# Turning twelve of sixteen row blocks by transposing DMA instead of on TensorE, in a fused LayerNorm + spectral filter + GeGLU kernel

## The chip, the cores and the metric

The kernel runs on one core of a Trainium2 chip. A core has five engines that run their own instruction streams and meet at semaphores: TensorE (PE, matmuls and transposes, results in PSUM), VectorE (DVE), ScalarE (ACT), GpSimd (POOL) and SyncE (SP, which here only issues DMA transfers). The metric is the device time of one execution in microseconds; three runs of the kernel before gave 176.29, 176.81 and 177.09 us.

## The reference

```python
xn = _layernorm(x, axis=-1)                       # x: (1, 2048, 512) bf16, eps 1e-5, no scale or bias
X  = rfft2(xn.astype(float32), axes=(-2, -1))     # over 2048 tokens and 512 features
y  = irfft2(X * (w_r + 1j * w_i), s=(2048, 512))  # w_r, w_i: (2048, 257)
g, u = xn @ w_gate, xn @ w_up                     # (512, 1792) each
h  = gelu_tanh(g) * u
out = x + y + h @ w_down                          # w_down: (1792, 512)
```

Two branches read the same normalised rows: a two-dimensional spectral filter and a gated MLP. Their results and x are added.

## The kernel before, in words

The 2048 tokens are 16 rows of 128 tokens (a "row" below is such a block, 128 tokens on the partitions by 512 features), and four rows make a chunk. For each row, VectorE takes the statistics (`stats`, lines 524 and 525), the reciprocal root of the variance comes from GpSimd (`root_pool`, lines 536 and 537; the first row's from ScalarE), and VectorE writes the normalised row into one of eight buffers in `specB` (`norm`, line 541). Roots are taken for four rows at a time from row 4 on.

Everything that follows wants the features on the partitions, so each normalised row is turned (`turn`, lines 543 to 559): TensorE transposes four 128x128 blocks per row into PSUM (line 554), and VectorE copies the result into `xnT` (line 559). From row 4 on two rows are turned at a time.

From `xnT` two things start. The MLP branch: `gated` makes, for a chunk and each of 14 blocks of hidden features, a gate group and an up group of four matmuls each (line 679); ScalarE takes gelu and a copy out of PSUM, VectorE multiplies (line 686), and `down` makes one row of output from 14 hidden blocks (line 724). The first chunk is done in smaller pieces at the start (`first`, line 698). The spectral branch: `fold` (VectorE) adds and subtracts mirrored features of a chunk, TensorE transforms pairs of rows along the features (line 593), ScalarE empties PSUM (line 598). When all four chunks are there, VectorE does the upper part of the token transform, TensorE the rest (lines 813 and 816), VectorE multiplies by the filter `W` in `filt` (line 472, with the edge columns at lines 826 and 860), and the inverse runs back the same way (lines 893, 894, 953) into x.

The filter comes from HBM in two halves: near rows, loaded straight from `w_r` and `w_i`, and mirror rows, which are first copied in reverse order from HBM into a scratch tensor in HBM (`w_mirror`) and then loaded from there. `tf` and `ti` are tables for the forward and inverse token transforms.

The order of instructions on each engine is written by a planner in the file (`_Sched`): every operation has an engine, a cost, a key or due time, and for transfers a size that is charged to one common pipe at `RATE`; the planner simulates and fixes each engine's order, and semaphore waits follow from what reads and writes what. So the orders of all engines shift when costs, keys or operations change. `STAT` and `NORM` set due times of statistics and norms of rows 4 to 15. Operations with a key over 1000, the MLP's matmuls, fill TensorE wherever nothing else is ready. `gate` is a list of operations that every later SyncE transfer must wait for.

All loads but three small ones go through SyncE's one queue, in this order: x, gate and up weights, small tables, the rest of x, `w_down`, `tf`, `ti`, the six reversing copies, the near filter rows, single rows of the filter, and the loads from the scratch.

Of the kernel before, what the change touches and what calls it, by code (L numbers as in the profile page):

```python
# [15 lines left out]
P = 128  # L16
NFC = 14
# [2 lines left out]
WARM = 8  # L20
HKEY = 1.5
NORM = 14.0, 1.5
STAT = 13.0, 1.6
SLACK = 0.05
MARGIN = 1.0
RATE = 340e3
# [120 lines left out]
class _Sched:  # L147
# [11 lines left out]
    def op(self, eng, cost, fn, reads=(), writes=(), tiles=(), key=0.0, after=(), dma=0, lag=0.0, due=None):  # L159
        o = _Op()  # L160
        o.eng, o.fn, o.cost, o.key, o.dma, o.lag, o.due = eng, fn, cost, key, dma, lag, due
        o.reads, o.writes, o.tiles = reads, writes, [(t, False) for t in tiles]
        o.extra = [a for a in after if a is not None]
        o.seq = len(self.ops)
        o.end = None
        o.pos = None
        self.ops.append(o)
        return o
# [182 lines left out]
def bass_parallel_sum__spectral_gfnet__glu_gated_geglu__prompt_kernel(  # L351
# [13 lines left out]
    c_ti = nc.inline_tensor(ti_np, name="c_ti")  # L365
# [9 lines left out]
    wdv = B_w_down.rearrange("(fc p) d -> p fc d", p=P)  # L375

    sch = _Sched()
    op = sch.op

    with ExitStack() as es:  # L380
        def sb(name, shape, dt=BF16, cell=0):
            n = int(np.prod(shape))
            t = es.enter_context(nc.sbuf_tensor(name, [P, n], dt))
            return view(t, name, 0, shape, cell)
# [14 lines left out]
        xnT = sb("xnT", [4, 4, 4, P])  # L399
        wg = sb("wg", [4, FF])  # L400
        wu = sb("wu", [4, FF])
        wd = sb("wd", [NFC, D])
        small = sb("smallc", [11, P])
        tf = sb("tokf", [18, P])
        ti = sb("toki", [8, 3, P])
        W = sb("filt", [2, 2, 8, 257], cell=1)
        w1 = sb("filt1024", [2, 512])
# [56 lines left out]
        gate = []  # L464

        def dma(q, dst, src, nbytes, wr=None, rd=None, key=0.0, after=(), cost=0.41, lag=0.0):
            after = tuple(after) + tuple(gate if q == "sp" else ())
            return op(q, cost, lambda e: e.dma_start(dst() if callable(dst) else dst.ap, src() if callable(src) else src.ap),  # L468
                      reads=rd if rd is not None else (), writes=wr if wr is not None else (), dma=nbytes, key=key, after=after, lag=lag)
# [7 lines left out]
        def load(q, dst, src, nbytes, **kw):  # L477
            return dma(q, dst, lambda: src, nbytes, wr=(dst,), **kw)
# [4 lines left out]
        k = iter(np.arange(0.0, 1.0, 0.001))  # L483
        first_row = None
        for s in range(4):
            for part, rows in halves(A_x, SL[s]):
                o = load("sp", x[part, s], rows, 1024 * (part.stop - part.start), key=next(k))
# [45 lines left out]
        def root_pool(s0, n, key):  # L533
            sl = slice(s0, s0 + n)
            v, y, h = vv[:, sl], rs[:, sl], half[:, sl]
            op("pool", 0.2 + 0.03 * n, lambda e: e.tensor_scalar(v.ap, bag.ap[:, sl, 1], LN_EPS, None, ADD), reads=(bag[:, sl],), writes=(v,), key=key)
            op("pool", 0.5 + 0.14 * n, lambda e: e.tensor_tensor(y.ap, v.ap, h.ap, ALU.pow), reads=(v, h), writes=(y,), key=key)

        def norm(s, key, due=None):
            o, i = xn(s).rs([512]), xs(s)  # L540
            op("dve", 0.34, lambda e: e.tensor_scalar(o.ap, i.ap, bag.ap[:, s, 0:1], rs.ap[:, s:s + 1], SUB, MUL),
               reads=(i, bag[:, s], rs[:, s:s + 1]), writes=(o,), key=key, due=due)

        def turn(s0, n, key):
            b, sl = s0 // 4, s0 % 4
            t = _T("sp")

            def bank():
                return ps_sp_bf[:, t.slot * 2048:t.slot * 2048 + 512 * n]

            def f(e):
                ins = None
                for i in range(4 * n):
                    ins = e.transpose(bank()[:, i * P:(i + 1) * P], xn(s0 + i // 4).ap[:, i % 4], ident.ap)  # L554
                return ins

            o = xnT[:, b, sl:sl + n].rs([512 * n])
            op("pe", 4 * n * 0.056, f, reads=tuple(xn(s0 + i) for i in range(n)) + (ident,), tiles=(t,), key=-40, lag=0.1)
            op("dve", 0.08 + n * 0.26, lambda e: e.tensor_copy(o.ap, bank()), writes=(o,), tiles=(t,), key=key)  # L559


        Y = R1(0, [16, D])
        H = R3(0, [16, D])
# [53 lines left out]
        fold(0)  # L617
        for s in range(4, 16):
            stats(s, 0.0, STAT[0] + STAT[1] * (s - 4))
            if s % 4 == 3:  # L620
                root_pool(s - 3, 4, -4.0)
        for s in range(4, 16):
            norm(s, 0.0, NORM[0] + NORM[1] * (s - 4))
            if s % 2 == 1:
                turn(s - 1, 2, 1.0)
            if s % 4 == 3:
                fold(s // 4)


        load("sp", wd, wdv, NFC * 131072, key=next(k))  # L630
        load("sp", tf, c_tf.ap().rearrange("p (t m) -> p t m", t=18), 589824, key=next(k))
        load("sp", ti, c_ti.ap().rearrange("p (v t q) -> p v t q", v=8, t=3), 786432, key=next(k))
        scr, far, near = {}, {}, {}
        for ri, src in ((0, A_w_r), (1, A_w_i)):
            c16 = src.rearrange("(m c) k -> c m k", c=16)
# [2 lines left out]
                dma("sp", lambda ri=ri: scr[ri][0:4], lambda c16=c16: c16[12:16, ::-1, :], 526336, key=next(k), cost=3.5, lag=6.0),  # L638
                dma("sp", lambda ri=ri: scr[ri][5:8], lambda c16=c16: c16[5:8, ::-1, :], 394752, key=next(k), cost=2.5, lag=6.0)]
            near[ri] = dma("sp", lambda ri=ri: scr[ri][4:9:4, 0:64], lambda c16=c16: c16[0:9:8, 127:63:-1, :], 131584, key=next(k), cost=2.0, lag=5.0)  # L640
        for ri, src in ((0, A_w_r), (1, A_w_i)):
            r16 = src.rearrange("(m c) k -> m c k", c=16)
            load("sp", W[0:64, ri, 0, 0], r16[0:64, 0], 32896, key=next(k))
            load("sp", W[64:P, ri, 0, 0], r16[0:64, 8], 32896, key=next(k))
            load("sp", W[:, ri, 0, 1], r16[:, 4], 65792, key=next(k))
            for c in (1, 2, 3):
                load("sp", W[:, ri, 0, 2 * c:2 * c + 2], r16[:, c:c + 9:8], 131584, key=next(k))
            load("sp", W[0:1, ri, 1, 0], r16[0:1, 0], 514, key=next(k))
        for ri in (1, 0):
            load("sp", W[1:64, ri, 1, 0], scr[ri][4, 0:63], 32382, after=(near[ri],), key=1.0 + next(k))  # L650
            load("sp", W[64:P, ri, 1, 0], scr[ri][8, 0:64], 32896, after=(near[ri],), key=1.0 + next(k))
            load("sp", W[:, ri, 1, 1], scr[ri][0], 65792, after=(far[ri][0],), key=1.0 + next(k))
            for c in (1, 2, 3):
                load("sp", W[:, ri, 1, 2 * c:2 * c + 2], scr[ri][4 - c::4][0:2].rearrange("c m k -> m c k"), 131584, after=tuple(far[ri]), key=1.0 + next(k))
        op("pool", 0.1, lambda e: e.memset(w1[0:1].ap, 0.0), writes=(w1,))
        for dst, src, lo, hi in ((w1[0:1, 0, 0:256], A_w_r, 0, 256), (w1[0:1, 0, 257:512], A_w_i, 1, 256),
                                 (w1[0:1, 1, 1:256], A_w_i, 1, 256), (w1[0:1, 1, 257:512], A_w_r, 1, 256),
                                 (w1[0:1, 1, 256:257], A_w_r, 256, 257)):
            load("sp", dst, src[1024:1025, lo:hi], 512, key=next(k))


        fill = [0]
# [143 lines left out]
        for v, hh in enumerate(((14, 15), (12, 13), (0, 1), (4, 6), (8, 9), (10, 11), (2, 7), (5, 3))):  # L806
            t = _T("sp")
# [17 lines left out]
        for ri, f in ((0, ADD), (1, SUB)):  # L825
            op("pool", 0.3, lambda e, ri=ri, f=f: e.tensor_tensor(edge.ap[:, ri], ev[0].ap[:, ri], ev[1].ap[:, ri], f),
               reads=(ev[0][:, ri], ev[1][:, ri]), writes=(edge[:, ri],), key=1.0)
# [53 lines left out]
        for v in range(8):  # L881
            t = _T("sp")

            def f_i(e, v=v, t=t):
# [15 lines left out]
               writes=(gv,), tiles=(t,), key=-0.5)  # L900
# [40 lines left out]
        for jq in range(4):  # L941
# [4 lines left out]
            for jp in (2 * jq, 2 * jq + 1):  # L946
                t = _T("sp")
# [57 lines left out]
```

## Time and profile before

| | before |
|---|---|
| time, median of 3 runs | 176.81 us (176.29 to 177.09) |
| the profiled execution | 177.05 us |
| its span | 175.3 us |
| TensorE busy | 170.2 us, 97% |
| VectorE busy | 146.4 us, 84% |
| ScalarE busy | 106.2 us, 61% |
| GpSimd busy | 11.3 us, 6% |
| granted TensorE clock | 1.00 |

The span runs from the first to the last instruction that the profiler saw; the execution's time holds 1.7 us around it. The chain of work that ended last is followed back from the last instruction, each time to what released it. In rows of groups and timelines, an operation is given as line, engine, operation, output<-input, shape; "<-" at the end names what ended the idle time before it. In a timeline the first two columns are start and duration in microseconds; neighbouring instructions of one kind are merged. SPq is SyncE's own queue of DMA issues; its durations are those of issuing, not of the transfers. In rows of windows, the columns are the window, its length, busy time and instruction count of TensorE, its weight loads, VectorE, ScalarE and GpSimd, then the granted clock, the busy share of the 16 DMA engines and GB/s.

### The profile page before, as it was taken

What the parts mean: (1) busy time and instruction counts of PE and PEld (TensorE: products, weight loads), DVE (VectorE), ACT (ScalarE), POOL (GpSimd) and SP (SyncE); (2) the same over time, 40 slices, a digit from 0 to 9 for tenths busy, and PEclk for the clock granted to TensorE, in tenths of its full rate; (3) what the DMA queues carried; (4) which work ended last, traced back from release to release, by engine and by line L of the source; (5) the groups of instructions that cost most, each with busy time, mean ns of one, the idle gap of its engine ahead of it and who ended that gap; (6) DMA issues with size and microseconds to landing.
All of it is one profiled execution on the core that took longest, in us unless ns stands there. A gap on an engine that the chain in (4) does not pass through costs nothing.

```text
span 175.3 us, 2759 instructions
## 1 busy us (share of the span) xinstructions
PE 170.2 (97%) x1042; PEld 89.8 (51%) x1042; DVE 146.4 (84%) x289; ACT 106.2 (61%) x172; POOL 11.3 (6%) x19
## 2 busy tenths in 40 slices
PE   7789999999999999999999999999999999999994
PEld 2578654555665444444444464554445564444443
DVE  3769999999819999976999999969999939982931
ACT  3378756567598375987636395794636896562000
POOL 2220302200000034000000000000000000000000
DMA  5999998222455530000000000000000001410311
GB/s 153 280 358 356 351 357 306 65 61 54 70 110 118 136 92 0 4 0 0 0 2 0 4 0 0 0 4 0 0 0 2 4 0 52 128 60 4 120 60 62
DMA packets 17805, 14.77 MB, mean 84 GB/s; under 512 B 1151, under 2 KB 17408, under 8 KB 17792
## 3 DMA queue, kind: packets, MB, share of 16 engines
q1 hardware_dynamic: 16592, 13.75, 26.7%
q10 hardware_dynamic: 1200, 0.85, 1.6%
q8 instruction: 8, 0.13, 0.3%
q14 instruction: 5, 0.04, 0.1%
HBM read 12.50 MB, written 3.15 MB: 89 GB/s over the span
## 4 chain that ended last, share of the span: by engine, by line
PE 92%; DMA 4%; SPq 1%; issue 0%; DVE 0%
PE ps_gu L679 54%; PE ps_dn L724 21%; PE ps_sp L724 7%; DMA wu<-in_B_w_up_dram 3%; PE ps_sp L593 3%; PE ps_sp L953 2%; PE ps_sp L554 2%; PE ps_sp L813 2%; DMA x_sb<-in_A_x_dram 1%; SPq L468 1%; PE ps_sp L893 1%; PE ps_sp L894 1%; PE ps_sp L816 0%; DVE x_sb L735 0%
## 5 line engine op out<-in xcount | busy, mean ns | idle before, releaser
L679 PE MATMUL ps_gu<-xnT,wu 128*128 128x512 bf16 (+1 forms) x236 | 56.7, 363 | 0.7 <-DMA wu<-in_B_w_up_dram 0.7
L679 PE MATMUL ps_gu<-xnT,wg 128*128 128x512 bf16 (+1 forms) x236 | 56.7, 363 | 0.0
L684 ACT ACTIVATE gg<-ps_gu 128x512 bf16<-128x512 f32 (+1 forms) x59 | 33.8, 573 | 13.8 <-PE ps_gu L679 12.5
L685 ACT ACTIVATE uu<-ps_gu 128x512 bf16<-128x512 f32 (+1 forms) x59 | 33.9, 575 | 12.8 <-PE ps_gu L679 12.3
L724 PE MATMUL ps_dn<-wd,hT 128*128 128x512 bf16 x168 | 38.9, 379 | 0.0
L679 PEld LDWEIGHTS ps_gu<-xnT,wu 128*128 128x128 bf16 x236 | 22.7, 98 | 22.9 <-ACT gg L684 0.9
L679 PEld LDWEIGHTS ps_gu<-xnT,wg 128*128 128x128 bf16 x236 | 22.6, 98 | 21.8 <-DVE xnT L559 0.3
L472 DVE TENSOR_TENSOR specB<-specB 128x1024 bf16<-128x1024 bf16 (+2 forms) x47 | 29.2, 659 | 1.5 <-ACT specB L958 1.4
L724 PEld LDWEIGHTS ps_dn<-wd,hT 128*128 128x128 bf16 x168 | 16.4, 98 | 19.6
L686 DVE TENSOR_TENSOR hT<-gg,uu 128x512 bf16<-128x512 bf16 (+1 forms) x59 | 22.3, 391 | 1.9 <-ACT uu L685 1.9
L732 ACT ACTIVATE db<-ps_dn 128x512 bf16<-128x512 f32 x12 | 7.2, 597 | 19.8 <-PE ps_dn L724 19.8
L472 DVE TENSOR_TENSOR specB<-specA 128x2048 bf16<-128x2048 bf16 x8 | 9.4, 1220 | 6.5 <-ACT specA L598 3.9
L524 DVE BATCH_NORM_STATS2 bst<-x_sb 128x6 f32<-128x512 bf16 x16 | 10.9, 682 | 3.8 <-DMA x_sb<-in_A_x_dram 3.6
L472 DVE TENSOR_TENSOR specC<-specB 128x1024 bf16<-128x1024 bf16 (+5 forms) x21 | 12.5, 628 | 0.1
L724 PE MATMUL ps_sp<-wd,hT 128*128 128x512 bf16 (+2 forms) x70 | 12.3, 336 | 0.0
L724 PEld LDWEIGHTS ps_sp<-wd,hT 128*128 128x128 bf16 x70 | 6.3, 98 | 6.1 <-DVE x_sb L735 0.2
L472 DVE TENSOR_TENSOR specB<-specB,filt 128x2048 bf16<-128x2048 bf16 x8 | 9.4, 1215 | 0.0
L821 ACT ACTIVATE specA<-ps_sp 128x1024 bf16<-128x1024 f32 x8 | 8.0, 1024 | 2.2 <-PE ps_sp L816 1.8
L733 DVE TENSOR_TENSOR x_sb<-db,x_sb 128x512 bf16<-128x512 bf16 x12 | 5.0, 415 | 4.4 <-ACT db L732 4.4
L958 ACT ACTIVATE specB<-ps_sp 128x1024 bf16<-128x1024 f32 x8 | 7.8, 1031 | 0.8 <-PE ps_sp L953 0.8
L598 ACT ACTIVATE specA<-ps_sp 128x1024 bf16<-128x1024 f32 x8 | 8.0, 1046 | 0.1
L899 ACT ACTIVATE specC<-ps_sp 128x1024 bf16<-128x1024 f32 x8 | 7.8, 1039 | 0.0
(64 smaller groups left out, 139.5 us busy)
## 6 DMA issues: line engine op xcount, KB each, us to landing
wd<-in_B_w_down_dram SPq DMA_DIRECT2D x1, 1792.0 KB, 13.4
out_dram<-x_sb SPq DMA_DIRECT2D x14, 128.0 KB, 1.8
x_sb<-in_A_x_dram SPq DMA_DIRECT2D x3, 512.0 KB, 8.4
wg<-in_B_w_gate_dram SPq DMA_DIRECT2D x2, 512.0 KB, 7.7
wu<-in_B_w_up_dram SPq DMA_DIRECT2D x2, 512.0 KB, 8.4
filt<-w_mirror SPq DMA_DIRECT2D x6, 128.5 KB, 2.5
toki<-c_ti SPq DMA_DIRECT2D x1, 768.0 KB, 9.5
tokf<-c_tf SPq DMA_DIRECT2D x1, 576.0 KB, 13.3
```

What stands on the lines that cost most here:

```text
L472: return op("dve", c_tt(n), lambda e: e.tensor_tensor(o.ap, a.ap, b.ap, f), reads=(a, b), writes=(o,), key=key, **kw)
L524: op("dve", 0.61, lambda e: e.bn_stats(bst[:, s].ap, xs(s).ap), reads=(xs(s),), writes=(bst[:, s],), key=key, due=due, after=after)
L598: op("act", c_act(1024), lambda e, yv=yv, t=t: e.activation(yv.ap, spair(t).rearrange("p (s r i) -> p s i r", s=4, r=4), ACT.Copy), writes ...
L679: ins = e.matmul(gub(t, n), w.ap[:, dc, fc * P:(fc + 1) * P], xnT.ap[:, b, sl, dc, :], start=(dc == 0), stop=(dc == 3))
L684: op("act", c_act(n), lambda e: e.activation(gg.ap[:, gs.slot, 0:n], gub(g, n), ACT.Gelu_apprx_tanh), tiles=(g, gs), key=0.0)
L685: op("act", c_act(n), lambda e: e.activation(uu.ap[:, us.slot, 0:n], gub(u, n), ACT.Copy), tiles=(u, us), key=0.0)
L686: op("dve", c_tt(n), lambda e: e.tensor_tensor(hT.ap[:, h.slot, lo:lo + n], gg.ap[:, gs.slot, 0:n], uu.ap[:, us.slot, 0:n], MUL), tiles=(g ...
L724: ins = e.matmul(bank(), hT.ap[:, hs[(b, fc)].slot, sl * P:(sl + 1) * P], wd.ap[:, fc, lo:lo + n], start=(fc == 0), stop=(fc == NFC - 1))
L732: op("act", c_act(n), lambda e: e.activation(db.ap[:, d.slot, 0:n], bank(), ACT.Copy), tiles=(t, d), key=0.0)
L821: op("act", c_act(1024), lambda e, xv=xv, t=t: e.activation(xv.ap, spair(t), ACT.Copy), writes=(xv,), tiles=(t,), key=-0.5)
L899: op("act", c_act(1024), lambda e, gv=gv, t=t: e.activation(gv.ap, spair(t).rearrange("p (k x i) -> p k x i", k=4, x=4), ACT.Copy), writes ...
L958: op("act", c_act(1024), lambda e, rv=rv, t=t: e.activation(rv.ap, spair(t), ACT.Copy), writes=(rv,), tiles=(t,), key=-0.5)
```

## The change

Rows 4 to 15 (chunks two to four) are no longer turned by TensorE and VectorE. A new function `turn_dma` issues, from SyncE, one transposing DMA for each row, from the normalised row in `specB` straight into `xnT`. Rows 0 to 3 are turned as before. The roots of rows 4 to 15 are taken for two rows at a time. The due times of the statistics lie closer together. On SyncE, `w_down` now has to come behind the norm of row 7, `tf`, the near rows and the single rows of the filter behind that of row 11, and the reversing copies, `ti` and the loads from the scratch, in this order, behind that of row 15.

```diff
-STAT = 13.0, 1.6
+STAT = 13.0, 1.2
...
+        def turn_dma(s):
+            i, o = xn(s), xnT[:, s // 4, s % 4]
+            op("sp", 1.25, lambda e: e.dma_start_transpose(o.ap, i.rs([512]).ap), reads=(i,), writes=(o,), dma=425000, key=-5.0)
...
         for s in range(4, 16):
             stats(s, 0.0, STAT[0] + STAT[1] * (s - 4))
-            if s % 4 == 3:
-                root_pool(s - 3, 4, -4.0)
+            if s % 2 == 1:
+                root_pool(s - 1, 2, -4.0)
+        hold = {}
         for s in range(4, 16):
             norm(s, 0.0, NORM[0] + NORM[1] * (s - 4))
-            if s % 2 == 1:
-                turn(s - 1, 2, 1.0)
+            hold[s] = sch.ops[-1]
+            turn_dma(s)
             if s % 4 == 3:
                 fold(s // 4)
 
-        load("sp", wd, wdv, NFC * 131072, key=next(k))
+        load("sp", wd, wdv, NFC * 131072, key=next(k), after=(hold[7],))
+        gate.append(hold[11])
         load("sp", tf, c_tf.ap().rearrange("p (t m) -> p t m", t=18), 589824, key=next(k))
-        load("sp", ti, c_ti.ap().rearrange("p (v t q) -> p v t q", v=8, t=3), 786432, key=next(k))
+        for ri, src in ((0, A_w_r), (1, A_w_i)):
+            r16 = src.rearrange("(m c) k -> m c k", c=16)
+            load("sp", W[0:64, ri, 0, 0], r16[0:64, 0], 32896, key=next(k))
...
+        op("pool", 0.1, lambda e: e.memset(w1[0:1].ap, 0.0), writes=(w1,))
...
+            load("sp", dst, src[1024:1025, lo:hi], 512, key=next(k))
+        gate.append(hold[15])
         scr, far, near = {}, {}, {}
...
-        for ri, src in ((0, A_w_r), (1, A_w_i)):
-            r16 = src.rearrange("(m c) k -> m c k", c=16)
...
+        load("sp", ti, c_ti.ap().rearrange("p (v t q) -> p v t q", v=8, t=3), 786432, key=next(k))
         for ri in (1, 0):
...
-        op("pool", 0.1, lambda e: e.memset(w1[0:1].ap, 0.0), writes=(w1,))
...
```

In the order that the planner writes, SyncE issues the turns of rows 4 to 7, `w_down`, the turns of rows 8 to 13, `tf`, the turns of rows 14 and 15, then the near and single rows, the reversing copies, `ti`, and the loads from the scratch.

More of the change, by code (lines that the diff above doesn't have):

```diff
@@ L619, in bass_parallel_sum__spectral_gfnet__glu_gated_geglu__prompt_kernel @@
             stats(s, 0.0, STAT[0] + STAT[1] * (s - 4))
-            if s % 4 == 3:
-                root_pool(s - 3, 4, -4.0)
+            if s % 2 == 1:
+                root_pool(s - 1, 2, -4.0)
+        hold = {}
         for s in range(4, 16):
             norm(s, 0.0, NORM[0] + NORM[1] * (s - 4))
-            if s % 2 == 1:
-                turn(s - 1, 2, 1.0)
+            hold[s] = sch.ops[-1]
+            turn_dma(s)
             if s % 4 == 3:
                 fold(s // 4)
-        load("sp", wd, wdv, NFC * 131072, key=next(k))
+        load("sp", wd, wdv, NFC * 131072, key=next(k), after=(hold[7],))
+        gate.append(hold[11])
         load("sp", tf, c_tf.ap().rearrange("p (t m) -> p t m", t=18), 589824, key=next(k))
-        load("sp", ti, c_ti.ap().rearrange("p (v t q) -> p v t q", v=8, t=3), 786432, key=next(k))
+        for ri, src in ((0, A_w_r), (1, A_w_i)):
+            r16 = src.rearrange("(m c) k -> m c k", c=16)
+            load("sp", W[0:64, ri, 0, 0], r16[0:64, 0], 32896, key=next(k))
+            load("sp", W[64:P, ri, 0, 0], r16[0:64, 8], 32896, key=next(k))
+            load("sp", W[:, ri, 0, 1], r16[:, 4], 65792, key=next(k))
+            for c in (1, 2, 3):
+                load("sp", W[:, ri, 0, 2 * c:2 * c + 2], r16[:, c:c + 9:8], 131584, key=next(k))
+            load("sp", W[0:1, ri, 1, 0], r16[0:1, 0], 514, key=next(k))
+        op("pool", 0.1, lambda e: e.memset(w1[0:1].ap, 0.0), writes=(w1,))
+        for dst, src, lo, hi in ((w1[0:1, 0, 0:256], A_w_r, 0, 256), (w1[0:1, 0, 257:512], A_w_i, 1, 256),
+                                 (w1[0:1, 1, 1:256], A_w_i, 1, 256), (w1[0:1, 1, 257:512], A_w_r, 1, 256),
+                                 (w1[0:1, 1, 256:257], A_w_r, 256, 257)):
+            load("sp", dst, src[1024:1025, lo:hi], 512, key=next(k))
+        gate.append(hold[15])
         scr, far, near = {}, {}, {}
@@ L640, in bass_parallel_sum__spectral_gfnet__glu_gated_geglu__prompt_kernel @@
             near[ri] = dma("sp", lambda ri=ri: scr[ri][4:9:4, 0:64], lambda c16=c16: c16[0:9:8, 127:63:-1, :], 131584, key=next(k), cost=2.0, lag=5.0)
-        for ri, src in ((0, A_w_r), (1, A_w_i)):
-            r16 = src.rearrange("(m c) k -> m c k", c=16)
[L643 to L648, printed above, removed]
+        load("sp", ti, c_ti.ap().rearrange("p (v t q) -> p v t q", v=8, t=3), 786432, key=next(k))
         for ri in (1, 0):
@@ L654, in bass_parallel_sum__spectral_gfnet__glu_gated_geglu__prompt_kernel @@
                 load("sp", W[:, ri, 1, 2 * c:2 * c + 2], scr[ri][4 - c::4][0:2].rearrange("c m k -> m c k"), 131584, after=tuple(far[ri]), key=1.0 + next(k))
-        op("pool", 0.1, lambda e: e.memset(w1[0:1].ap, 0.0), writes=(w1,))
[L656 to L659, printed above, removed]
         fill = [0]
```

## The prediction

> **What bounds the kernel.** I read the page first, then the chain of work that ended last in order of time, then the groups by line and shape, and then the timelines of SyncE, VectorE and GpSimd around the rows that are turned.
>
> ```profile
> span 175.3 us, 2759 instructions
> ...
> PE 170.2 (97%) x1042; PEld 89.8 (51%) x1042; DVE 146.4 (84%) x289; ACT 106.2 (61%) x172; POOL 11.3 (6%) x19
> ...
> PE 92%; DMA 4%; SPq 1%; issue 0%; DVE 0%
> ```
>
> TensorE is busy for 97% of the span and makes up 92% of the chain. The rest is the start, before the first weights are there, and the last store. So a microsecond of TensorE work that goes away is a microsecond of time, as long as nothing that TensorE needs comes later than before. The chain, where it passes the turns (line 554):
>
> ```profile
> 23.51 0.45 PE ps_sp L554 x8
> 23.96 0.86 PE ps_gu L679 x4
> 24.82 0.45 PE ps_sp L554 x8
> 25.27 6.04 PE ps_gu L679 x28
> 31.31 0.89 PE ps_sp L554 x16
> 32.20 6.04 PE ps_gu L679 x28
> 38.25 0.89 PE ps_sp L554 x16
> 39.14 2.59 PE ps_gu L679 x12
> 41.73 1.32 PE ps_sp L593 x16
> ...
> 43.91 3.02 PE ps_dn L724 x14
> ```
>
> No idle time lies between the pieces. A gate or up group (4 matmuls) takes 0.863 us (6.04 for 7), a block of forward transforms of two row pairs (16 matmuls, line 593) 1.32, a down row (14 matmuls) 3.02, and 48 transposes 0.45 + 0.45 + 0.89 + 0.89 = 2.68.
>
> **Taken off TensorE.** All 48 transposes of chunks two to four go: -2.68 us, in the path. This is the one gain that I count. The first four rows keep their 16 transposes.
>
> **Taken off VectorE.** The copies out of PSUM go with them:
>
> ```profile
> L559 DVE COPY xnT<-ps_sp 128x1024 bf16<-128x1024 bf16 x6 | 3.9, 669 | 0.0
> ```
>
> VectorE loses 3.9 us of work beside TensorE's path. It is worth nothing in the time by itself; what it does is to bring the normalised rows (line 541) forward.
>
> **When the rows are normalised.** The norms of rows 4-7, 8-11 and 12-15 and the folds behind them, before:
>
> ```profile
> 21.58 1.37 DVE L541 TENSOR_SCALAR specB<-x_sb,bag,rstd 128x512 bf16<-128x512 bf16 x4
> 28.57 1.38 DVE L541 TENSOR_SCALAR specB<-x_sb,bag,rstd 128x512 bf16<-128x512 bf16 x4
> 35.33 1.37 DVE L541 TENSOR_SCALAR specB<-x_sb,bag,rstd 128x512 bf16<-128x512 bf16 x4
> 42.57 1.28 DVE L472 TENSOR_TENSOR specB<-xnT 128x1024 bf16<-128x1024 bf16 x2
> 44.98 0.74 DVE L472 TENSOR_TENSOR specB<-specB 128x512 bf16<-128x512 bf16 x2
> 45.98 1.28 DVE L472 TENSOR_TENSOR specC<-specB 128x1024 bf16<-128x1024 bf16 x2
> ```
>
> In the changed order four copies (0.6 each by their pitch) and about 1 us of products and fold steps no longer stand ahead of the last norm: 36.7 - 3.4 = 33.3. By the same count row 7 ends at 22.1 and row 11 at 28.5. Rows 4 and 5, whose root no longer waits for four rows, come at about 17.5. The six roots by two on GpSimd instead of three by four cost nothing: it is 6% busy.
>
> **Added on SyncE: twelve turning transfers, 128 KB each.** Each waits for its norm with the whole SyncE queue behind it: w_down behind row 7, the forward table behind row 13, the filter rows behind row 15. The transfers share one queue with the loads. SyncE and the queue, before:
>
> ```profile
> 14.34 1.42 SPq L468 DMA_DIRECT2D wd<-in_B_w_down_dram  x1
> 15.80 5.68 SPq L468 DMA_DIRECT2D tokf<-c_tf  x1
> 21.52 0.75 SPq L468 DMA_DIRECT2D toki<-c_ti  x1
> 22.31 10.98 SPq L468 DMA_DIRECT2D w_mirror<-in_A_w_r_dram  x3
> 33.34 10.16 SPq L468 DMA_DIRECT2D w_mirror<-in_A_w_i_dram  x3
> 43.54 6.68 SPq L468 DMA_DIRECT2D filt<-in_A_w_r_dram  x7
> 50.27 4.19 SPq L468 DMA_DIRECT2D filt<-in_A_w_i_dram  x7
> ...
> 55.67 1.91 SPq L468 DMA_DIRECT2D filt<-w_mirror  x4
> ...
> 57.98 3.98 SPq L468 DMA_DIRECT2D filt<-w_mirror  x8
> ```
>
> ```profile
> L468 SPq DMA_DIRECT2D x_sb<-in_A_x_dram x8: 328/474/1314, 0.7 to 13.0; - x8
> ...
> DMA to landing us min/median/max: 1.4/1.8/9.5
> ```
>
> ```profile
> wd<-in_B_w_down_dram SPq DMA_DIRECT2D x1, 1792.0 KB, 13.4
> ...
> filt<-w_mirror SPq DMA_DIRECT2D x6, 128.5 KB, 2.5
> ```
>
> ```profile
> 20.00:24.00 4.00, 4.00 (x26) 2.01 (x24) 3.62 (x12) 2.84 (x5) 0.88 (x1) 1.00 1.10 349
> 24.00:28.00 4.00, 4.00 (x26) 2.10 (x25) 4.00 (x13) 2.04 (x5) 0.74 (x2) 1.00 1.08 384
> 36.00:40.00 4.00, 4.00 (x32) 2.29 (x31) 4.00 (x10) 2.08 (x4) 0.00 (x0) 1.00 0.29 64
> ...
> 60.00:64.00 4.00, 4.00 (x20) 1.84 (x19) 3.94 (x10) 3.19 (x5) 0.51 (x1) 1.00 0.63 151
> ```
>
> (The last two columns are the DMA engines' share and GB/s.) The last chunk of x, issued at 13.0, lands 9.5 later: the queue is free for turns from 22.5.
>
> No row shows a turning transfer. Call p the time that one takes of the queue. Below: 131,072 bytes at the 384 GB/s of the window from 24 give 0.34 us. Above: the reversing copies into the mirror run at 64 GB/s in the window from 36, which gives 2.05. The 151 GB/s of the short filter rows at 60 to 64 give 0.87. I take 1.25: it lies between the short rows and the reversing copies, the two transfers that are nearest in kind, and it is what the planner in the file charges (425,000 bytes at its 340 GB/s, and 1.25 us of SyncE). Its other charges fit the rows: 0.34 per norm against 1.37 for four, 8 x 0.056 for a turn against 0.45.
>
> With w_down at 1.835 MB / 349 GB/s = 5.2 us, the forward table at 0.59 MB = 1.7, and about 1.0 from the last byte to the signal (the 2.5 of a 128.5 KB filter copy, less 0.87 of data and half a microsecond of issue), the queue runs: four turns, w_down, six turns, table, two turns. Against that stand TensorE's needs in the changed order, counted on from 23.51, up to which both orders are alike:
>
> - Chunk two's first gate group stands 11 groups later: 23.51 + 9.5 = 33.0. Its rows land at 22.5 + 4p + 1.0 = 28.5. In time; row 4's buffer, which row 12's norm overwrites near 29.5, is also free.
> - Chunk three: landed at 28.7 + 8p = 38.7, and the folds to its first half transform take 1.28 + 0.74 + 0.64 = 2.7 more: 41.4. TensorE comes to it after 19 groups, one transform block and half a down row, 23.51 + 16.4 + 1.32 + 1.51 = 42.7. In time.
> - Chunk four: landed at 30.4 + 12p = 45.4, folded at 48.1. TensorE is there after 22 groups, two blocks and one down row: 23.51 + 18.99 + 2.64 + 3.02 = 48.2. Just in time.
> - w_down lands at 22.5 + 5 + 5.2 + 1 = 33.7 and is first wanted at 23.51 + 16.4 + 1.32 = 41.2.
>
> So at 1.25 the plan closes with 0.1 us to spare; at p > 1.26 TensorE stalls by 12 x (p - 1.26) at the forward transforms of chunk four. If SyncE's issue is the slow part and the queue is quick, the last issue is 17.4 + 12c + 2.2 (w_down and table) and c may reach about 2.0.
>
> The Trainium skill, "DMA: Bandwidth & Descriptors", section "Latency and other measured facts", gives 261 GB/s for a transposing DMA with a non-contiguous middle dimension. By an estimate from that page p would be 0.50, no turn would be late, and the sum would stay at the 2.68 gained; no run here shows that rate yet.
>
> **Moved on SyncE: the filter.** The near rows now go ahead of the mirrors and the mirror copies stay last, but all of it starts only behind row 15's turn. At 1.25 per issue, from row 7's turn at 23.5, SyncE is at 23.5 + 1.4 + 7.5 + 0.75 + 2.5 = 35.7. Then 14 near rows (2 x 4.19 without backlog), five single-row pieces (1.6 by the gaps that the quoted rows leave at 54.5 and 57.6), mirrors 21.1, inverse table 0.75, copies 5.9: 73.4, landed 2.5 later at 75.9. The edge columns follow on GpSimd, and the product needs them here:
>
> ```profile
> 64.19 3.46 POOL L826 TENSOR_TENSOR edge<-filt 128x16 bf16<-128x16 bf16 x1 [2.76 <-DMA filt<-w_mirror]
> ```
>
> ```profile
> 80.28 2.36 DVE L472 TENSOR_TENSOR specB<-specA 128x2048 bf16<-128x2048 bf16 x2 [2.49 <-ACT specA L821]
> 82.56 0.26 DVE L860 TENSOR_TENSOR edge<-specA,edge 128x16 bf16<-128x16 bf16 x2
> ```
>
> 75.9 + 3.5 = 79.4 at worst, against 82.56 less about 1.2 (TensorE's last forward product by groups of the changed order) = 81.4. Costed at nothing; the cover is 2.0 us. If SyncE is held up by a full queue for 4 us more, VectorE waits 2.0.
>
> **Sum.** The profiled execution took 177.05 us (span 175.3), 0.24 above the median of 176.81. 177.05 - 2.68 = 174.37; I add 0.4 for the 0.1 and 2.0 us covers being thin, which gives 174.8, and less the 0.24 the median of the changed kernel should be 174.5.
>
> **Rivals.**
>
> *The turns are late (slower).* Place: the wait of the forward transforms of chunk four (line 593 before) for the fold of chunk four, and of that fold for the transfers. Decides at p = 1.26 + 2.68/12 = 1.48. At the mirror's 64 GB/s, p = 2.05: 12 x 0.79 = 9.5 of stall, 176.8 - 2.7 + 9.5 = 183.6; at p = 1.7, 179.4. For it: a transpose scatters what it reads, as the reversing copies do, and those are the slowest transfers of the trace. Against: those copies use a small share of the engines (0.29 in their window), and a transfer of 128 rows need not. Chance 0.26.
>
> *The turns don't overlap (slower still).* If each transfer begins only when the one before has landed, p is the 2.5 us that a 128.5 KB copy takes alone: 12 x 1.24 = 14.9, 189. Against: the loads of the trace overlap freely on one queue. Chance 0.05. The Trainium skill, "VectorE: DVE Perf Modes", section "The three transpose paths", speaks against the change: 1309 ns for a 128x128 block by DMA and 390 on TensorE, with the advice to use TensorE where PSUM will do. This trace disagrees for TensorE, where eight blocks take 0.45 us in the chain, 56 ns each. By the page's figure four blocks end to end would be 5.2 us a row, and by an estimate from it the time would be about 221.
>
> *The filter is late.* VectorE waits for the edge columns ahead of the product, TensorE at the inverse products some 1.5 us after that. With 4 to 7 us of extra hold-up on SyncE, 0.5 to 3.5 us of stall: 174.6 to 177.6. For it: the forward table's issue was held 5.68 us behind w_down in the same queue. Chance 0.11.
>
> *The change does nothing that can be told* (p near 1.48, or small waits of TensorE on folds that eat 2 us): 176.8. Chance 0.05.
>
> **Chances and range.** The forecast, turns and filter in time or late by less than 1 us (173.9 to 175.5), has 0.53. About 0.5% (0.9 us) is what a measurement can tell. Faster by more than that: the forecast, half of the filter's case and a little of the late turns, 0.59. Within: 0.09. Slower: 0.32. Since cases of both signs hold the chance, the range for 8 in 10 is 173.8 to 183.0, up to p = 2.0; above lie the rest of the late turns and the turns that don't overlap.
>
> **What would show it.** Right: no line-554 pieces behind 13 us in the chain, no DVE copies of 128x1024, twelve turning issues on SyncE at 1.3 us or less, TensorE without a wait at the transforms near 48 us, POOL's second edge over before 81. Wrong: TensorE waiting there for VectorE, and VectorE's fold for a transfer into xnT; or VectorE waiting for edge columns near 81 us.

## The result, and the profile after

The changed kernel takes 174.28 us in the median of four executions (173.99 to 174.76), against 176.95 for the kernel before, measured beside it (176.29 to 178.30, four executions). The ratio is 0.985 (0.981 to 0.9889): 2.67 us less. 174.5 was forecast.

The page of the changed kernel, the lines that answer to those shown of before:

```profile
span 172.2 us, 2683 instructions
...
PE 167.9 (98%) x994; PEld 87.1 (51%) x994; DVE 143.3 (83%) x283; ACT 106.2 (62%) x172; POOL 11.8 (7%) x25
...
PE 93%; DMA 4%; ACT 1%; DVE 1%; issue 0%; DVEq 0%
```

TensorE has 48 instructions fewer and 2.3 us less to do, and is still what the chain consists of. The chain of the changed kernel in order of time, through the stretch in which the rows were turned (line 686 is the gate and up groups, 597 the forward transforms, 731 the down rows):

```profile
13.32 23.62 PE ps_gu L686 x132
36.94 1.32 PE ps_sp L597 x16
38.26 2.59 PE ps_gu L686 x12
40.85 1.51 PE ps_dn L731 x7
42.36 1.32 PE ps_sp L597 x16
43.69 1.51 PE ps_dn L731 x7
45.20 2.59 PE ps_gu L686 x12
47.78 1.32 PE ps_sp L597 x16
```

The pieces of line 554 are gone, each piece starts where the one before ends, and no transform waits. So the 48 transposes came out of the path at their full length.

The profiled execution took 173.99 us, 3.06 less than that of before; the medians differ by 2.67. What goes beyond the 2.68 lies at the start. There TensorE of the kernel before waited once for weights, as the list of its waits says (total, times, longest):

```profile
PE ps_gu L679 <- DMA wu<-in_B_w_up_dram: 0.7, 1, 0.7
```

In the profiled execution of the changed kernel those weights came in time. The change does not touch them.

SyncE's timeline of the changed kernel (start, length, what, how many):

```profile
16.94 6.16 SPq L563 DMA_TRANSPOSE xnT<-specB  x4
23.14 0.58 SPq L468 DMA_DIRECT2D wd<-in_B_w_down_dram  x1
25.35 10.13 SPq L563 DMA_TRANSPOSE xnT<-specB  x6
35.52 0.58 SPq L468 DMA_DIRECT2D tokf<-c_tf  x1
36.15 2.54 SPq L563 DMA_TRANSPOSE xnT<-specB  x2
38.73 4.36 SPq L468 DMA_DIRECT2D filt<-in_A_w_r_dram  x7
...
48.55 6.20 SPq L468 DMA_DIRECT2D w_mirror<-in_A_w_r_dram  x3
54.80 9.80 SPq L468 DMA_DIRECT2D w_mirror<-in_A_w_i_dram  x3
```

and the tile that is turned into (shortest, median and longest ns of one issue):

```profile
L563 SPq DMA_TRANSPOSE xnT<-specB x12: 1188/1280/2376, 16.9 to 37.4; - x12
```

An issue holds SyncE for 1.28 us in the median, and the last one ends at 38.69. VectorE's timeline has the last norm (row 15) and the folds of chunks three and four:

```profile
33.25 0.41 DVE L541 TENSOR_SCALAR specB<-x_sb,bag,rstd 128x512 bf16<-128x512 bf16 x1
...
37.12 1.29 DVE L472 TENSOR_TENSOR specB<-xnT 128x1024 bf16<-128x1024 bf16 x2
...
41.86 1.28 DVE L472 TENSOR_TENSOR specB<-xnT 128x1024 bf16<-128x1024 bf16 x2
...
43.85 0.69 DVE L472 TENSOR_TENSOR specC<-specB 128x1024 bf16<-128x1024 bf16 x1
```

No fold waits for a transfer: behind none of these rows stands an idle time. The first half of chunk four is folded at 44.5 (43.85 + 0.69), and TensorE asks for it at 47.78.

### The profile page after: what moved, and what is told of

Read it like the earlier page. It is cut to its first block, busy times and chain, and to the rows that moved or that the text cites. A ratio compares the mean times of both kernels' runs of the same rounds, so it can differ in the third digit from the quotient of the medians.

```text
span 172.2 us, 2683 instructions
## 1 busy us (share of the span) xinstructions
PE 167.9 (98%) x994; PEld 87.1 (51%) x994; DVE 143.3 (83%) x283; ACT 106.2 (62%) x172; POOL 11.8 (7%) x25
## 4 chain that ended last, share of the span: by engine, by line
PE 93%; DMA 4%; ACT 1%; DVE 1%; issue 0%; DVEq 0%
PE ps_gu L686 55%; PE ps_dn L731 21%; PE ps_sp L731 7%; DMA x_sb<-in_A_x_dram 4%; PE ps_sp L597 3%; PE ps_sp L960 2%; PE ps_sp L820 2%; PE ps_sp L900 1%; PE ps_sp L901 1%; ACT gg L716 1%; PE ps_sp L823 1%; DVE bst L524 0%; PE ps_gu L705 0%; PE ps_sp L554 0%; ACT uu L717 0%
## 5 line engine op out<-in xcount | busy, mean ns | idle before, releaser
L686 PE MATMUL ps_gu<-xnT,wu 128*128 128x512 bf16 (+1 forms) x236 | 56.7, 363 | 0.2 <-ACT gg L716 0.2
L686 PE MATMUL ps_gu<-xnT,wg 128*128 128x512 bf16 (+1 forms) x236 | 56.7, 363 | 0.0
L686 PEld LDWEIGHTS ps_gu<-xnT,wu 128*128 128x128 bf16 x236 | 22.7, 98 | 22.9 <-ACT gg L716 0.4
L472 DVE TENSOR_TENSOR specB<-specB 128x1024 bf16<-128x1024 bf16 (+2 forms) x47 | 29.3, 662 | 1.5 <-ACT specB L965 1.4
L731 PE MATMUL ps_sp<-wd,hT 128*128 128x512 bf16 (+2 forms) x70 | 12.3, 336 | 0.0
L828 ACT ACTIVATE specA<-ps_sp 128x1024 bf16<-128x1024 f32 x8 | 8.0, 1024 | 1.6 <-PE ps_sp L820 1.3
```

Source lines behind the costliest of these rows:

```text
L472: return op("dve", c_tt(n), lambda e: e.tensor_tensor(o.ap, a.ap, b.ap, f), reads=(a, b), writes=(o,), key=key, **kw)
L686: ins = e.matmul(gub(t, n), w.ap[:, dc, fc * P:(fc + 1) * P], xnT.ap[:, b, sl, dc, :], start=(dc == 0), stop=(dc == 3))
L731: ins = e.matmul(bank(), hT.ap[:, hs[(b, fc)].slot, sl * P:(sl + 1) * P], wd.ap[:, fc, lo:lo + n], start=(fc == 0), stop=(fc == NFC - 1))
L828: op("act", c_act(1024), lambda e, xv=xv, t=t: e.activation(xv.ap, spair(t), ACT.Copy), writes=(xv,), tiles=(t,), key=-0.5)
```

## The experiments

The theory was that of the prediction: 2.68 us of TensorE's time are the whole gain, and everything else only has to keep up. Rivals: that VectorE's six copies, or earlier norms, bring the gain; that the turns or the filter were close to being late; and that the roots by two and the order of the filter rows were not needed.

### The 48 transposes put back on TensorE, beside the transfers

The transposes write to PSUM and nothing reads them. The copies stay out.

```
+        def turn_idle(s0, n):
+            t = _T("sp")
...
+                    ins = e.transpose(ps_sp_bf[:, at:at + P], xn(s0 + i // 4).ap[:, i % 4], ident.ap)
...
+            op("pe", 4 * n * 0.056, f, reads=tuple(xn(s0 + i) for i in range(n)) + (ident,), tiles=(t,), key=-40, lag=0.1)
...
             turn_dma(s)
+            if s % 2 == 1:
+                turn_idle(s - 1, 2)
```

> The changed kernel with the 48 transposes of rows 4 to 15 put back on TensorE, into PSUM that nobody reads, beside the turning transfers that still fill xnT; no copies on VectorE. Theory (the gain is TensorE time and nothing else): 174.28 + 2.68 = 176.96, the same as before within 0.5%. Rival (the gain is VectorE's copies, or the earlier norms): the time stays at 174.3.

Measured: 176.89 us, ratio to before 1.0007 (0.9987 to 1.0027); the kernel before took 176.71 in that round. The gain is gone, as far as the interval can tell. VectorE's 3.9 us and the earlier norms, which this kernel keeps, bring nothing by themselves.

### Two thirds of the turns by transfer

Chunk two is turned on TensorE, chunks three and four by transfers.

```
-            turn_dma(s)
+            if s >= 8:
+                turn_dma(s)
+            elif s % 2 == 1:
+                turn(s - 1, 2, 1.0)
```

> Rows 8 to 15 are turned by transfers, rows 4 to 7 by TensorE as before. Theory (0.0559 us of TensorE per block and nothing else): 32 of the 48 transposes go, 176.95 - 1.79 = 175.2. Rival (the gain comes with the first turned chunk, from an earlier start of chunk two): 176.9; rival (it comes with the last): 174.3.

Measured: 175.08, ratio 0.9918 (0.9894 to 0.9941), against 0.985 (0.981 to 0.9889) with all. 32 of the 48 transposes should give 1.8 us. The median lies 1.6 below the 176.71 that the kernel before took in that round, and the interval of the ratio goes from 1.0 to 1.9 us: it agrees with 1.8, and can't tell more.

### All turns back on TensorE, the rest of the change kept

```
-            turn_dma(s)
+            if s % 2 == 1:
+                turn(s - 1, 2, 1.0)
```

> Everything of the change but the turns: roots by two, closer statistics, the new order of the filter and the holds on SyncE, while rows 4 to 15 are turned by TensorE and copied by VectorE as before. Theory: these parts only make room, 176.95 within 0.5%. Rival (the roots by two and the new order bring part of the gain by themselves): 175.0 to 176.0.

Measured: 177.30, ratio 1.0034 (1.0016 to 1.0051). The roots by two, the earlier near rows and the later mirrors cost 0.6 us by the ratio when nothing is turned by transfers. They bring nothing by themselves. Whether the room that they were to make is needed, the last experiments ask.

### VectorE's time put back, the transposes left out

Six additions of two normalised rows each, into memory that the inverse table takes later, stand in for the six copies. The result is not used.

```
             turn_dma(s)
+            if s % 2 == 1:
+                d, a = ti.rs([3, 1024])[:, (s // 2) % 3], RB(8192 + 512 * ((s - 1) % 8), [1024])
+                tt(d, a, a, ADD, 1024, 1.0)
```

> The changed kernel with six additions of 128x1024 put back on VectorE (0.68 us each, as long as the copies were), on the normalised rows, results unused. Theory (VectorE's copies were beside the path): 174.3 within 0.5%. Rival (VectorE's 3.9 us count): up to 178.2.

Measured: 176.31, ratio 0.9967 (0.9945 to 0.9989). The expectation of 174.3 missed by 2.0 us. But the planner had charged the additions and moved other work too: row 15's turn went behind the near filter rows, and a fold waited 3.43 us for it. So the same additions were made again at no charge in the plan, which leaves SyncE's and TensorE's orders as they are in the changed kernel:

```
+            if s % 2 == 1:
+                d, a = ti.rs([3, 1024])[:, (s // 2) % 3], RB(8192 + 512 * ((s - 1) % 8), [1024])
+                op("dve", 0.0, lambda e, d=d, a=a: e.tensor_tensor(d.ap, a.ap, a.ap, ADD), reads=(a,), writes=(d,), key=1.0)
```

> The six additions of 128x1024 on VectorE again, but now charged at nothing in the planner, so that the orders of SyncE, TensorE and ScalarE stay those of the changed kernel (in the first form the planner had put row 15's turn behind the near filter rows). Theory (what cost 2.0 us was the place of row 15's turn on SyncE, not VectorE's time): chunk four's fold starts some 3 us later, inside its cover: 174.3 to 174.9. Rival (VectorE's 4 us cost it, through norms and folds that come later): 176.0 to 176.6.

Measured: 176.67, ratio 0.9988 (0.9965 to 1.0011): no change from before that can be told, though TensorE has none of the 48 transposes. The theory falls. The busy times from 30 to 40 us (TensorE, weight loads, VectorE, ScalarE, GpSimd, then the clock, the DMA share and GB/s), first of the changed kernel, then of this one:

```profile
30.00:40.00 10.00, 10.00 (x58) 5.12 (x56) 9.96 (x25) 7.73 (x12) 1.31 (x2) 1.00 1.04 199
```

```profile
30.00:40.00 10.00, 8.22 (x44) 3.68 (x43) 10.00 (x26) 5.30 (x11) 1.66 (x3) 1.00 0.99 195
```

VectorE is full in both. With the additions it is TensorE that idles, 1.8 of 10 us. Waits in this kernel (line 689 is the groups, 694 the gate's activation, 696 VectorE's product):

```profile
ACT gg L694 <- DVE hT L696: 4.5, 5, 1.5
...
PEld ps_gu L689 <- ACT gg L694: 2.7, 5, 0.8
...
PEld ps_sp L597 <- DVE specC L472: 1.7, 1, 1.7
```

and the first of them in the changed kernel:

```profile
ACT gg L691 <- DVE hT L693: 0.8, 1, 0.8
```

VectorE's products come late, so ScalarE cannot write the next activation, so PSUM does not come free for the next group; and the folds come late for a transform. Of the 30 us from 14 to 44, VectorE is busy for 29.3 here, for 29.6 in the kernel before and for 28.3 in the changed kernel. Taking 2.68 us from TensorE needed time taken from VectorE beside it. Neither alone gives the gain: 176.89 and 176.67. (The first form, in which the planner moved other work around the additions, kept 0.6 us by its ratio.)

The additions do not stand exactly where the copies stood, and so how much of the wait each single one makes is open. That VectorE as a whole is the limit is what the two windows and the waits show.

### The last four turns doubled

Rows 12 to 15 are turned twice, the second time into memory that is free. That asks how near chunk four is to being late.

```
+            if s >= 12:
+                d = ti.rs([6, 4, P])[:, (s - 4) % 6]
+                op("sp", 0.0, lambda e: e.dma_start_transpose(d.ap, i.rs([512]).ap), reads=(i,), writes=(d,), dma=1, key=-5.0)
```

> Only the turns of rows 12 to 15 are issued twice. Theory (cover of 3.3 us at chunk four): row 15's turn is issued 3 x 1.28 = 3.8 us later, the fold of chunk four follows by as much less what it now waits beyond the landing, TensorE stalls by 0.5 to 1.5: 174.8 to 175.8, with a wait at the forward transforms near 48 us. Rival (cover of 0.1 us, as predicted at p = 1.25): 178. Rival (a much larger cover): 174.3.

Measured: 174.21, ratio 0.9849 (0.9828 to 0.987). The stall that was expected did not come. SyncE's last turn into the folded tile, and VectorE's fold that waited for it:

```profile
41.39 1.27 SPq L563 DMA_TRANSPOSE xnT<-specB  x1
```

```profile
44.15 1.29 DVE L472 TENSOR_TENSOR specB<-xnT 128x1024 bf16<-128x1024 bf16 x2 [2.06 <-DMA xnT<-specB]
```

The turn's issue ends at 42.66, 4.0 later than in the changed kernel, the fold starts 1.5 behind that, and is 2.3 later than there (44.15 against 41.86). TensorE had 3.2 us to spare (44.54 against 47.78) and notices nothing. The last turn of the changed kernel, and the time from the start of its issue to its landing:

```profile
L563 SPq DMA_TRANSPOSE xnT<-specB x1: 1294/1294/1294, 37.4 to 37.4; - x1
...
DMA to landing us min/median/max: 3.5/3.5/3.5
```

It lands at 40.9, 1.1 us behind the forward table that stands ahead of it in the queue (issued at 35.52, landed 4.3 later), and 1.0 ahead of its fold. So the whole room is about 4.2 us, and the last landing here is 3.2 later, not 4.0.

### All turns doubled

```
+            if s >= 4:
+                d = ti.rs([6, 4, P])[:, (s - 4) % 6]
+                op("sp", 0.0, lambda e: e.dma_start_transpose(d.ap, i.rs([512]).ap), reads=(i,), writes=(d,), dma=1, key=-5.0)
```

> Each of the twelve turning transfers is issued twice, the second into a place that is loaded over later. The profile of the changed kernel shows 1.28 us of SyncE per turn. Theory (SyncE's issue sets the pace, and the cover of chunk four's fold is about 3.3 us: folded at 44.5, wanted at 47.8): twelve more issues of 1.28 less the gaps of some 3 us in which SyncE waited put the last landing near 53 and chunk four's fold near 56, TensorE stalls by 7 to 9 us, 181 to 183. Rival (turning is far from any limit): under 175. Rival of the prediction (the queue is the slow part at p = 1.25, doubled to 2.5): 12 x 1.24 = 15 us, 189.

Measured: 185.42, ratio 1.049 (1.0437 to 1.0543), 2.4 us above the top of what was expected. TensorE's timeline at the transforms of chunks three and four, with the wait in brackets, and the granted clock in the windows behind (the third number from the end):

```profile
45.56 1.49 PE L600 MATMUL ps_sp<-smallc,specC 128*128 128x128 bf16 x16 [3.24 <-DVE specC L472]
...
50.13 1.03 PE L689 MATMUL ps_gu<-xnT,wg 128*128 128x512 bf16 x4
56.71 2.74 PE L600 MATMUL ps_sp<-smallc,specC 128*128 128x128 bf16 x16 [5.55 <-DVE specC L472]
```

```profile
44.00:48.00 4.00, 2.44 (x22) 1.77 (x23) 2.74 (x7) 1.57 (x2) 0.00 (x0) 1.00 0.49 98
```

```profile
52.00:56.00 4.00, 0.00 (x0) 0.00 (x0) 2.01 (x5) 0.00 (x0) 0.00 (x0) 0.82 0.58 109
56.00:58.00 2.00, 1.29 (x9) 1.05 (x10) 1.92 (x4) 0.00 (x0) 0.00 (x0) 0.50 0.72 174
...
60.00:64.00 4.00, 4.00 (x27) 2.39 (x26) 2.71 (x4) 3.09 (x5) 0.00 (x0) 0.83 0.52 121
```

The stalls are 3.24 us at the transforms of chunk three and 5.55 at those of chunk four, 8.8 together: the late turns that the prediction named as its first rival. The span is 183.5, 11.3 above 172.2, so 2.5 are left. They are the clock: behind the 5.55 us of idle it is granted at half, and the block of 16 takes 2.74 us in place of 1.49. A clock of 0.83 over the four microseconds from 60 means half speed for another 1.4 of them, so TensorE ran at half from 56.7 to about 61.4, which loses 2.35 us. Behind the 3.24 us wait the clock stayed at 1.00.

### Two rows in one transfer

Six transfers of two rows (eight 128 x 128 blocks) in place of twelve of one.

```
+        def turn_two(s):
+            i, o = RB(8192 + 512 * (s % 8), [1024]), xnT[:, s // 4, s % 4:s % 4 + 2].rs([8, P])
+            op("sp", 2.5, lambda e: e.dma_start_transpose(o.ap, i.ap), reads=(i,), writes=(o,), dma=850000, key=-5.0)
...
-            turn_dma(s)
+            if s % 2 == 1:
+                turn_two(s - 1)
```

> Six transfers that turn two rows each (eight blocks) in place of twelve. Theory (SyncE's 1.28 us is a price per block, 0.32): about 2.5 us per issue, time 174.3 within 0.5%, since the second row of a pair was the later one anyway. Rival (a price per transfer): 1.3 to 1.5 us per issue, SyncE through with the turns some 5 us sooner, time 174.3 as well; the issue row tells the two apart.

Measured: 173.97, ratio 0.9833 (0.9807 to 0.9859). The six issues on SyncE (shortest, median and longest ns, start of the first and the last):

```profile
L563 SPq DMA_TRANSPOSE xnT<-specB x6: 1237/1906/3137, 17.0 to 34.5; - x6
```

The shortest issue of eight blocks takes 1.24 us, the shortest of four 1.19. So the least price on SyncE is paid by the transfer, not by the block: by the block it would be 2.4. The median of the six is longer than with four blocks (1.91 against 1.28), and so is the longest (3.14 against 2.38); that these were held up by the loads ahead of them is likely, and not shown. SyncE is through at 35.8 in place of 38.7; the time is the same within what these runs can tell, since nothing waited for SyncE.

### Rows 2 and 3 by transfer too

```
-            turn(s, 1, -50.0)
+            turn_dma(s)
```

> Rows 2 and 3, too, are turned by transfers (56 blocks off TensorE in all). Theory (the queue serves in order and is full of loads until 22 us): both rows land only near 20 us or later, TensorE wants them near 12.5, stalls by 7 to 9 us against 0.45 gained: 181 to 183. Rival (a turn overtakes the loads and lands 4.2 us after its issue, as the median in the changed kernel): near 16, a stall of 3 us: 177. Rival (enough other work): 173.8.

Measured: 185.26, ratio 1.0478 (1.0447 to 1.051). TensorE's last group ahead of its wait and the first behind it, its clock in the window from 14, and SyncE's timeline:

```profile
12.26 0.60 PE L686 MATMUL ps_gu<-xnT,wu 128*128 128x256 bf16 x4
22.68 1.03 PE L686 MATMUL ps_gu<-xnT,wg 128*128 128x256 bf16 x4 [9.82 <-DMA xnT<-specB]
```

```profile
14.00:20.00 6.00, 0.00 (x0) 0.00 (x0) 2.69 (x8) 0.00 (x0) 1.85 (x4) 0.85 1.09 354
```

```profile
12.21 1.69 SPq L468 DMA_DIRECT2D x_sb<-in_A_x_dram  x2
13.94 11.43 SPq L563 DMA_TRANSPOSE xnT<-specB  x6
```

The two turns are issued from 13.94, behind the last megabyte of x in the same queue, and TensorE gets them at 22.7. The queue serves what was issued first. The 9.8 us are the loss, with the half clock behind them: 0.50 up to 28 us and a mean of 0.97 from 28 to 36, so until about 28.5, 5.8 us long, which loses another 2.9. Less 0.45 gained that makes 12.3; the span is 12.0 longer than the changed kernel's. Turning by transfer is worth doing only for rows that are wanted after the loads ahead of them have drained.

### The reversing copies ahead of the near rows

The changed kernel's near and single rows go back behind the reversing copies. The lines that make the copies are moved up as they are.

```
+        gate.append(hold[15])
+        scr, far, near = {}, {}, {}
...
         for ri, src in ((0, A_w_r), (1, A_w_i)):
             r16 = src.rearrange("(m c) k -> m c k", c=16)
...
-        gate.append(hold[15])
-        scr, far, near = {}, {}, {}
...
```

> The near rows and the single rows of the filter go behind the reversing copies again; the orders of TensorE and VectorE are those of the changed kernel. Theory (the edge columns are ready at 76.4 and wanted at about 81, a cover of 4.7 us): 174.3 within 0.5%. Rival (the new order of the filter was needed): the near rows are held up behind the reversing copies, the last copies land 5 to 6 us later, and TensorE stalls: 175.3 to 177.

Measured: 174.05, ratio 0.9841 (0.982 to 0.9862), the same as the changed kernel. GpSimd has the edge columns at 76.1 (72.36 + 3.72):

```profile
72.36 3.72 POOL L833 TENSOR_TENSOR edge<-filt 128x16 bf16<-128x16 bf16 x2 [39.46 <-DMA filt<-w_mirror]
```

Which of the two comes first behind the turns does not matter here.

### Roots by four again, and the place of the last turns

First the roots by four, as before, with their due times:

```
-STAT = 13.0, 1.2
+STAT = 13.0, 1.6
...
-            if s % 2 == 1:
-                root_pool(s - 1, 2, -4.0)
+            if s % 4 == 3:
+                root_pool(s - 3, 4, -4.0)
```

> The turns by transfers, but roots by four rows and the statistics at the old spacing. Theory (SyncE needs 1.28 us per turn, and four rows that become ready together put all four issues behind the last root): the turns start 2 to 4 us later and use up the cover of 3.3 us at chunk four; 174.3 to 175.5. Rival (roots by two are needed, or the plan breaks): 177 and more. Rival (no matter at all): 174.3 with chunk four's fold no later than 42.

Measured: 178.82, 180.47, 182.74 and 183.07; the ratio of the two shortest is 1.0156 (1.0102 to 1.0211). SyncE, and VectorE's fold of chunk four, in the execution of 178.82:

```profile
36.66 4.83 SPq L468 DMA_DIRECT2D filt<-in_A_w_r_dram  x7
...
46.95 5.15 SPq L563 DMA_TRANSPOSE xnT<-specB  x4
```

```profile
53.38 0.69 DVE L472 TENSOR_TENSOR specB<-xnT 128x1024 bf16<-128x1024 bf16 x1 [5.00 <-DMA xnT<-specB]
```

The roots are not late by 9 us. In the changed order the planner has the four turns of chunk four issued behind the near rows, which hold SyncE for 10 us. So the same kernel was run with those rows held back behind row 15's norm:

```
         gate.append(hold[11])
...
+        gate.append(hold[15])
         for ri, src in ((0, A_w_r), (1, A_w_i)):
             r16 = src.rearrange("(m c) k -> m c k", c=16)
...
-        gate.append(hold[15])
```

> Roots by four and statistics at the old spacing as in the kernel that took 181.6, with one line more: the near rows of the filter, too, wait for row 15's norm, so that SyncE issues the turns of rows 12 to 15 ahead of the filter. Theory (that kernel lost its time because chunk four's turns stood behind 10 us of filter loads on SyncE): turns through by about 42, landed by 43.5, folded by 46.2, wanted at 47.8: 174.3 to 175.0. Rival (roots by four make the turns too late wherever they stand): 177 and more.

Measured: 173.97, ratio 0.9847 (0.9818 to 0.9875). SyncE:

```profile
36.92 5.13 SPq L563 DMA_TRANSPOSE xnT<-specB  x4
42.10 4.35 SPq L468 DMA_DIRECT2D filt<-in_A_w_r_dram  x7
```

With the turns ahead of the near rows, roots by four are as good as roots by two. What decides is what the turns stand behind on SyncE. Why the four executions of the kernel with the turns behind lie so far apart is open: only the shortest has a trace, and in it the clock is 1.00 throughout. The others had mean clocks of 0.99, 0.981 and 0.981. The kernel with all turns doubled had 0.981 too, from a long wait and the half clock behind it, so the same is likely here; no trace shows it.

The two kernels at 173.97 are 0.3 below the changed kernel's 174.28, with intervals of the ratio that overlap; no version was found that is surely better than it.

## Why the prediction was right

**TensorE's 2.68 us.** Right: 2.67 between the medians, none of it left when the transposes come back (176.89), and a part that agrees with two thirds of it with two thirds of the turns (175.08).

**"It is worth nothing in the time by itself."** True to the letter, and the weak step all the same. Taking VectorE's copies off brings nothing alone, but without it the 2.68 us are not there either: 176.67. The sentence that failed stands at the head of the prediction: a microsecond of TensorE is a microsecond of time as long as nothing comes *later* than before. When TensorE gets shorter by 2.7 us, all that feeds it must come *earlier* by as much. The prediction worked out the new needs for the turned rows, for w_down and for the edge columns, but not for the products and folds of VectorE. Its own windows had the warning: 4.00 busy of 4.00 at 24 and at 36 us. The number came out because the 3.9 us taken off VectorE are more than the 2.68 taken off TensorE. That was never weighed; in this the prediction was lucky.

**The norms.** Row 15's norm ends at 33.66; 33.3 was forecast.

**The turns.** The price taken, 1.25, is near the 1.28 measured, but it was meant for the queue, and it is SyncE's. The prediction kept both open: TensorE was to stall from 1.26 on for the one, and from about 2.0 on for the other. The queue's own price shows where turns stand behind loads. The first and the fourth turn of the changed kernel, issued behind x:

```profile
L563 SPq DMA_TRANSPOSE xnT<-specB x1: 1731/1731/1731, 16.9 to 16.9; - x1
...
DMA to landing us min/median/max: 6.7/6.7/6.7
```

```profile
L563 SPq DMA_TRANSPOSE xnT<-specB x1: 1188/1188/1188, 21.9 to 21.9; - x1
...
DMA to landing us min/median/max: 3.2/3.2/3.2
```

They land at 23.6 and 25.1: three turns in 1.5 us, 0.5 each, though each issue took 1.19 us or more. So p is about 0.5 and not 1.25, and the turns were limited by SyncE and by what stood ahead of them in the queue. That queue did run in order, as the prediction had it: w_down lands at 31.9 (23.14 + 8.8), the turn behind it at 32.4; the forward table at 39.8 (35.52 + 4.3), the last turn at 40.9. The landing of chunk four had been put at 45.4, the first half of its fold at 48.1; that came at 44.5. The cover was 3.2 us where 0.1 was counted, and so the 0.4 that was added for thin covers was not spent: 174.5 against 174.28. The bounds from 0.34 to 2.05 hold the value; the rate of the reversing copies is not that of a turn.

The Trainium skill, "DMA: Bandwidth & Descriptors", section "Latency and other measured facts", has 261 GB/s, by the prediction's estimate 0.50 for the queue. The trace agrees: 0.5. The Trainium skill, "VectorE: DVE Perf Modes", section "The three transpose paths", has 1309 ns for a block. Laid end to end, as in the prediction's estimate of 221 us for the kernel, that does not hold here: turns of four blocks land 0.5 us apart. No run here turns a single block.

**Turns that are late.** The rival was wrong at this size, and its mechanism was right. Doubling all turns gives 5.55 us of stall at just the place named, and 3.24 more at chunk three. The rival that transfers don't overlap is wrong: turns that wait in the queue land 0.5 us apart, while each takes 3.2 us or more from the start of its issue to its landing.

**The filter.** In time, with 4.6 us of cover where 2.0 was counted. GpSimd's second edge and VectorE's use of the edges in the changed kernel:

```profile
76.21 0.23 POOL L833 TENSOR_TENSOR edge<-filt 128x16 bf16<-128x16 bf16 x1 [0.33 <-DMA filt<-w_mirror]
```

```profile
81.07 0.26 DVE L867 TENSOR_TENSOR edge<-specA,edge 128x16 bf16<-128x16 bf16 x2
```

Two terms were off in opposite ways. SyncE was through with the turns at 38.7, where 35.7 was counted. The mirrors took 16.0 us of SyncE (6.20 + 9.80), where 21.1 was carried over from before: there the first three were issued into a queue that was still busy with w_down and two tables. SyncE's length of an issue includes, it seems, the hold-up by what is queued ahead, and must not be carried to another place.

## What to carry to other kernels

Before work is taken off the engine that bounds a stage, look at the busy time of the others in that stage: an engine that is full beside it becomes the bound at once. In the runs here the gain was the smaller of the two reliefs. Test it by putting the time of each engine back alone. A transfer that takes over an engine's work is free only as long as it lands before its data are wanted. What decides that is what stands ahead of it, in the queue and on the issuing engine: read both from the issues and their landings. Doubling the transfer tells how much room there is.

## What the runs showed of the hardware

A turning transfer within the core's memory holds SyncE for 1.19 us at the least for 128 x 512 and 1.24 for 128 x 1024, against 0.58 for the issue of w_down in the changed kernel; the longest issues, among loads, took 2.4 and 3.1 us. Behind loads the turns land in the order of their issue, 0.5 us apart for 128 KB each. With its queue empty (the last turn of the kernel with roots by four and the turns ahead, issued at 40.8) a turn lands 2.5 us after the start of its issue, some 1.2 after its end.

Idle time of TensorE costs more than itself beyond some length. The 3.24 us wait left the clock at 1.00; behind those of 5.55 and 9.82 us TensorE ran at 0.50 for 4.7 and 5.8 us, some 2.4 and 2.9 us of loss on top. The Trainium skill, "TensorE: Matmul & The Clock Gate", section "HAM oscillation — how this bites in real kernels", warns of idle gaps above about 3.4 us. The traces agree, as far as 3.24 and 5.55 can tell. But the drop does not come at one fixed time: with all turns doubled, a mean of 0.82 in the window from 52 means half speed from 54.6 on, 3.4 us after TensorE's last matmul at 51.2; with rows 2 and 3 by transfer, a mean of 0.85 in the window from 14 to 20 means half speed from 18.2 on, 5.3 us after its last matmul at 12.9.
